# Four head pairs of the first batch: keys transposed unscaled, their inverse norm given to the exponential

## The chip, the core and the metric

The kernel runs on one core of one Trainium2 chip. The metric is the device time of one launch in microseconds (us); 597.22 us is the median of five runs of the kernel before. The core has a matrix engine (TensorE, PE in the profile; PEld is its weight load), a vector engine (VectorE, DVE), a scalar engine (ScalarE, ACT), GpSimd (POOL) and SyncE (SP). Each works through its own instructions in order; semaphores make one wait for another. POOL and SP issue the DMA transfers here.

## What is computed

Cosine attention over 8 batches, 12 heads, 448 tokens and 64 numbers a head, followed by a mixer: a low-rank mix over the tokens and a two-layer perceptron of width 3072.

```python
q_n = q / (norm(q) + 1e-06);  k_n = k / (norm(k) + 1e-06)
attn = softmax(q_n @ k_n.T / tau)            # tau = 0.1
x = (attn @ v) as [8, 448, 768]
u = x + (x.T @ U @ V).T                      # rank 32 over the tokens
out = u + relu(u @ w_ch1) @ w_ch2
```

## The kernel before

The work is planned at build time. `Plan` (L100) holds a list of operations, each with an engine, an estimated duration, what it depends on, the buffer slots that it takes and gives back, and a priority. `plan.run` (L153) plays them in estimated time, and the order in which they come out is the order in which the instructions stand on each engine. So a different duration or priority in one place can reorder the engines' instructions elsewhere. PE and POOL have streams whose order is kept; ACT, DVE and SP take the ready operation of lowest priority number. Where the plan sees PE idle, the last loop (L963) puts in small matmuls on a dummy tile (`warm_up`, L547), which compute nothing that is used.

Heads go in pairs, six to a batch. For each group of heads:

- `load_qk` (L463) brings q and k from HBM, cast to bf16, with the 448 tokens laid out as 112 partitions x 4 chunks. For batch 0 there are four groups: heads 0-1 (float32, through SP, L906), heads 2-3, 4-7 and 8-11 (through POOL, L909 to L913). `load_v` (L472) brings v in four transfers. On POOL the order is heads 2-3, 4-7, the identity matrix for transposing, v, heads 8-11, then weights.
- `squares` (L482) squares q and k on ACT or DVE (L495, L497) and DVE sums each row of 64 (L501).
- `scales` (L508) makes 1/(norm + eps): ACT takes Ln (L514) and Exp of half of it (L517), DVE adds eps (L520) and takes the reciprocal (L522).
- `norm` (L552) multiplies q and k by it on DVE (L564, into `xn`), PE transposes both in `flip` (L434; four transposes of 112x128 for q, four for k, L446), and ACT or DVE copies the transposed tiles to `qkT` (L852, L854).
- `attention` (L585): per pair four chunks of 112 keys. For each, PE computes two score matmuls, one per head (L599), into two PSUM banks; one Exp over both, 896 wide, with the constant scale 1/tau, writes `attn` (L605). When all four are there, 32 matmuls per pair multiply with v (L619); v carries a column of ones, so the row sums come along. DVE divides (L626, L628) into X. `attn` has two buffers.

When batch 0's attention is complete, `stage0` and `columns` (L662, L640) do the low-rank mix and the transposition to `uT` (L676, L650, L655), and `mlp` (L767) starts with the matmuls of L788 and then L822. The first layer of batch 0 waits for the last exponential of batch 0 (L791). From then on, the perceptron's matmuls of one batch fill PE around the attention of the following batches.

U and V of the mix are loaded in float32 through SP after the first pair is normalised (L876, L922), and cast to bf16 on POOL (L882, L885). POOL's casts stand in its queue ahead of the q and k loads of batch 1.

Of the kernel before, what the change touches and what calls it, by code (L numbers as in the profile page):

```python
# [12 lines left out]
BF = mybir.dt.bfloat16  # L13
# [8 lines left out]
PAD = 64  # L22
# [234 lines left out]
def kernel(  # L257
# [24 lines left out]
    G = 4  # L282
    inv_tau = 1.0 / float(tau)
    EPS = 1e-6
    PE_BATCHES = 2
    LATE, VLATE = 8.0, 3.2
    BURST = 2
    FILL = 0.7

# [19 lines left out]
    xn_t = fixed(3, [SCH, 2 * SC, 128], BF, "xn")  # L309
    attn_t = fixed(2, [SCH, SC, 2, 512], BF, "attn")  # L310
    v_t = fixed(2, [SCH, H, SC, D + 2], BF, "v_nat")
# [73 lines left out]

    plan = Plan()
    pe_warm = plan.stream("PE")
    pe_tp = plan.stream("PE")
# [72 lines left out]
    last_av = {}  # L461

    def load_qk(b, h0, h1, ld=None, lo=0, uses=None):  # L463

        ld = ld or Slot(r_ld, 4 if uses is None else uses)
        ops = [load(lambda i=i, src=src: nc.gpsimd.dma_start(  # L466
            out=ld.tile[:, i, lo:lo + h1 - h0, :],
            in_=src[b, h0:h1].rearrange("h (s c) d -> s h (c d)", c=SC)),
            (h1 - h0) * (0.31 if b else 0.35) + (1.2 if b == 0 and h0 == 4 and i == 0 else 0.0), acq=[ld], late=2.5 if b == 0 else LATE) for i, src in enumerate((q, k))]
        return ld, ops, lo  # L470

    def load_v(b):  # L472

        old = [last_av.get((b - 2, p)) for p in range(NPAIR)]
        ops = [load(lambda c=c: nc.gpsimd.dma_start(  # L475
            out=v_t[b % 2][:, :, c, 0:D],
            in_=v[b].rearrange("h (s c) d -> c s h d", c=SC)[c]),
            SCH * H * (0.001 if b else 0.0009), deps=old, late=LATE if b else VLATE) for c in range(SC)]
        for h in range(H):
            got[b, h, "v"] = ops  # L480
# [27 lines left out]
    def scales(b, h0, h1, ld, ops, lo, ii, inv, pr, on, hold=(), then=()):  # L508

        g = h1 - h0  # L510
        ss, ln, nv = Slot(r_ss, 1), Slot(r_ln, 1), Slot(r_ln, 1)
        red = squares(b, g, ld, ops, lo, ii, ss, pr, on, hold, then)
        w = slice(ii[0], ii[-1] + 1)
        o = plan.add(Op("ACT", 0.25, lambda: nc.scalar.activation(  # L514
            ln.tile[:, w, 0:g, :], ss.tile[:, w, 0:g, :], AF.Ln),
            deps=red, acq=[ln], rel=[ss], prio=0))
        up = o = plan.add(Op("ACT", 0.2, lambda: nc.scalar.activation(  # L517
            nv.tile[:, w, 0:g, :], ln.tile[:, w, 0:g, :], AF.Exp, scale=0.5),
            deps=[o], acq=[nv], rel=[ln], prio=0))
        o = plan.add(Op("DVE", 0.21, lambda: nc.vector.tensor_scalar_add(  # L520
            nv.tile[:, w, 0:g, :], nv.tile[:, w, 0:g, :], EPS), deps=[o], prio=pr))
        o = plan.add(Op("DVE", 0.27, lambda: nc.vector.reciprocal(  # L522
            inv.tile[:, w, 0:g, :], nv.tile[:, w, 0:g, :]), deps=[o], acq=[inv], rel=[nv], prio=pr))
        return o, up

    def stats(b, h0, h1, ld, ops, lo, hold=(), then=()):

        pr = 0.3 + 0.03 * h0 if b == 0 else 4
        inv = Slot(r_inv, h1 - h0)
        o, _ = scales(b, h0, h1, ld, ops, lo, (0, 1), inv, pr, "DVE" if b else "ACT/DVE", hold, then)  # L530
        for p in range(h0 // 2, h1 // 2):
            o_ = norm(b, p, ld, lo + 2 * p - h0, inv, 2 * p - h0, {0: o, 1: o}, pr)
        return o_

    def stats_first(ld, ops):

        inv = Slot(r_inv, 2)
        done, ups = {}, []
        for i in range(2):
            done[i], up = scales(0, 0, 2, ld, ops, 0, (i,), inv, -1 - 0.1 * i, "ACT")  # L540
            ups.append(up)
        return ups + norm(0, 0, ld, 0, inv, 0, done, -1)

# [7 lines left out]

    def norm(b, p, ld, la, inv, a, deps, pr):  # L552


        by_pe = b < PE_BATCHES
        first = b == 0 and p == 0
        xn, qkT = Slot(r_xn, 2 if by_pe else 1), Slot(r_qkT, SC // (1 if b == 0 else BURST))

        def part(i):
            def fn():  # L560
                src = ld.tile[:, i, la:la + 2, :].rearrange("p h (c d) -> p h c d", d=D)
                sc = inv.tile[:, i, a:a + 2, :].unsqueeze(3).to_broadcast([SCH, 2, SC, D])
                dst = xn.tile[:, SC * (1 - i):SC * (2 - i), :].rearrange("p c (h d) -> p h c d", h=2)
                nc.vector.tensor_mul(dst, src, sc)  # L564
            return plan.add(Op("DVE", dve_t(512), fn, deps=[deps[i]], acq=[xn],
                               rel=[getattr(ld, "slot", ld), inv], prio=pr))

        ops = {i: part(i) for i in ((0, 1) if first else (1, 0))}
        if not by_pe:
            done = [plan.add(Op("SP", 0.1, lambda: nc.sync.dma_start_transpose(  # L570
                out=qkT.tile, in_=xn.tile.rearrange("p b e -> p (b e)")), deps=list(ops.values()), acq=[qkT],
                rel=[xn], prio=0, lat=("x", 0.05 * 56, LATE)))]
        else:
            done = []
            for i, o in ops.items():
                b0, b1 = SC * (1 - i), SC * (2 - i)
                done.append(flip(
                    pe_tp, [(lambda z=z: xn.tile[:, z, :]) for z in range(b0, b1)], SCH,
                    lambda: qkT.tile, (lambda t_, x, b0=b0, b1=b1: [(t_[:, b0:b1, :], x)]),
                    [o], [qkT], [xn], 1, "ACT/DVE", 0.05))  # L580
        got[b, p, "qkT"] = (qkT, done)
        return list(ops.values())


    def attention(b, p, X):  # L585
        off = PAD * (b % 2)
        qkT, qdeps = got.pop((b, p, "qkT"))
        attn = Slot(r_attn, 2)
        exps = []
        g = 1 if b == 0 else BURST  # L590
        for c0 in range(0, SC, g):
            scs = [Slot(r_sc, 1) for _ in range(g)]

            def score(scs=scs, c0=c0):
                flat = qkT.tile.rearrange("p b s -> p (b s)")
                for n, sc in enumerate(scs):
                    for hh in range(2):
# [5 lines left out]
                            deps=qdeps, acq=scs, rel=[qkT]), pe_first if b == 0 else pe_sc)  # L603
            for n, sc in enumerate(scs):
                exps.append(plan.add(Op("ACT", act_t(2 * S, 0.08), lambda sc=sc, c=c0 + n: nc.scalar.activation(  # L605
                    out=attn.tile[:, c, :, off:off + S], in_=sc.tile[0:SCH, :, 0:S], func=AF.Exp,
                    scale=inv_tau), deps=[o], acq=[attn], rel=[sc], prio=0.1 if b == 0 else 1)))
        last_exp[b] = exps[-1]
# [256 lines left out]
    warm_set = fill(lambda: nc.vector.memset(warm_t, 1.0), 128, prio=-20)  # L865
    plan.add(Op("PE", 5.4, lambda: warm_up(52), deps=[warm_set], acq=[warm]), pe_warm)
    attn_set = [fill(lambda t_=t_: set_attn(t_), 1000, prio=i - 2.5) for i, t_ in enumerate(attn_t)]
# [13 lines left out]
    def cast_u(par):  # L881
        nc.gpsimd.tensor_copy(out=U_sb[:, par], in_=U_f()[:, par])  # L882

    def cast_v():
        nc.gpsimd.tensor_copy(out=V_sb[:, PAD:PAD + S].rearrange("r (c s) -> r c s", c=SC),  # L885
                       in_=V_f().rearrange("r (s c) -> r c s", c=SC))
# [11 lines left out]
    def att(b):  # L898
        X = Slot(r_X, 0) if b else X0
        muls = [] if b else list(muls0)  # L900
        for p in range(0 if b else 1, NPAIR):
# [8 lines left out]
    third = load_qk(0, 4, 8)  # L910
    id_set = plan.add(Op("POOL", 0.8, lambda: make_identity(nc, ident)), pool_q)
    load_v(0)
    fourth = load_qk(0, 8, 12)  # L913
    v_set = [fill(lambda: set_v(v_t[0]), 1000, prio=-1.4)]
# [3 lines left out]
    begun_2 = stats(0, 2, 4, *second, hold=begun[:2], then=begun)  # L918
    z = fill(lambda: nc.vector.memset(V_sb, 0.0), 500, prio=3, deps=begun)
    zf = fill(lambda: nc.vector.memset(U_f(), 0.0), 400, prio=0.5, acq=[uv], deps=begun)  # L920
    u0 = load_u(0)
# [7 lines left out]
    v_set.append(fill(lambda: set_v(v_t[1]), 1000, prio=3, deps=late))  # L929
    consts = [plan.add(Op("POOL", 0.4, lambda: cast_u(0), deps=u0 + [z], rel=[uv]), pool_q),  # L930
              plan.add(Op("POOL", 1.2, cast_v, deps=v0 + [z], rel=[uv]), pool_q),
              plan.add(Op("POOL", 0.4, lambda: cast_u(1), deps=u1 + [z], rel=[uv]), pool_q)]
    state[0] = att(0)
# [29 lines left out]
    for o in order:  # L963
        if o.by == "PE" and not cool:
            if free is not None and o.start - free > 0.25:
                warm_up(int((o.start - free - 0.12) * FILL / 0.056))
            free, cool = o.start + o.dur, warm in o.rel
        for s in o.acq:
            if s.tile is None and not getattr(s, "own", False):
                s.tile = s.ring.make(s.group if isinstance(s.ring, BankRing) else s.i)  # L970
        o.fn()
# [33 lines left out]
```

## Time and profile before

| what | value |
|---|---|
| five runs | 597.95, 597.39, 596.33, 596.21, 597.22 us; median 597.22 |
| the profiled execution's own time | 595.37 us |
| its span in the profile | 593.6 us |
| PE busy | 585.7 us (99%) |
| DVE / ACT / POOL busy | 308.2 (52%) / 270.2 (46%) / 75.9 us (13%) |
| dummy matmuls (L550) | 195, of which 188 start before 32 us |
| granted TensorE clock | 1.00 |

In what follows a timeline line reads: start, time taken, engine, line of the code, operation, tile written <- tiles read, how often; in brackets, the idle time of the engine before it and what ended it. A line that stands for several instructions in a row gives the time from the first start to the last end. A line of windows gives the stretch and its length and then, for each engine, busy microseconds and the number of instructions. A busy PE says little by itself: matmuls overlap, and the dummy ones count.

### The profile page before, as it was taken

The numbers are of one execution on the slowest core, as the hardware profiler recorded it, in microseconds if no ns is written. First come the engines' busy times: TensorE is split into PE (matmuls) and PEld (weight loads), VectorE is DVE, ScalarE is ACT, GpSimd is POOL, SyncE is SP. The second block draws the span as 40 slices with busy tenths as digits, with TensorE's granted clock in tenths as the row PEclk, the third lists the DMA queues.
The fourth block names the chain that finished last, engine by engine and source line by source line (L and its number), as shares of the span: only waits on it lengthen the run. The fifth ranks groups of instructions, "written<-read, shape, count | busy, mean of one in ns | idle before, by whom it ended". The sixth has DMA issues, their size and how long they took to land.

```text
span 593.6 us, 11746 instructions
## 1 busy us (share of the span) xinstructions
PE 585.7 (99%) x4920; PEld 333.2 (56%) x4920; DVE 308.2 (52%) x729; ACT 270.2 (46%) x425; POOL 75.9 (13%) x101
## 2 busy tenths in 40 slices
PE   8999999999999999999999999999999999999997
PEld 7665655444555555554445655465445666554565
DVE  7969949999987768658772442224221210110011
ACT  7777753566555576447661156505631025014300
POOL 6354220040400210130020000000000000000000
PEclk9999999999999999999999999999999999999999
DMA  9999993897996595695494131121002110510021
GB/s 152 196 190 188 210 167 76 129 141 93 110 153 121 76 96 90 129 136 77 48 78 95 42 59 32 41 67 29 1 1 66 45 37 0 94 41 0 1 55 53
DMA packets 132852, 50.68 MB, mean 85 GB/s; under 512 B 97728, under 2 KB 132800, under 8 KB 132800
## 3 DMA queue, kind: packets, MB, share of 16 engines
q0 software_dynamic: 71680, 25.73, 38.9%
q1 hardware_dynamic: 61056, 24.19, 20.8%
q8 instruction: 38, 0.62, 0.4%
q14 instruction: 14, 0.11, 0.1%
q10 hardware_dynamic: 64, 0.02, 0.0%
HBM read 52.25 MB, written 11.01 MB: 107 GB/s over the span
## 4 chain that ended last, share of the span: by engine, by line
PE 93%; DVE 3%; POOL 1%; DMA 1%; ACT 1%; issue 0%; DVEq 0%; POOLq 0%
PE bank L788 38%; PE bank L822 37%; PE bank L619 8%; PE bank L599 7%; PE bank L712 2%; DMA qk_nat<-in_q_dram 1%; DVE xn L564 1%; ACT attn L605 1%; PE bank L676 1%; PE bank L446 1%; POOL v_nat L475 1%; POOL qk_nat L466 0%; DVE ss L501 0%; DVE u_nat L726 0%; DVE O_sb L831 0%
## 5 line engine op out<-in xcount | busy, mean ns | idle before, releaser
L788 PE MATMUL bank<-uT,w_sb 128*128 128x512 bf16 (+1 forms) x1152 | 232.9, 353 | 0.2 <-ACT uT L852 0.2
L822 PE MATMUL bank<-w_sb,relu 128*128 128x384 bf16 (+1 forms) x1368 | 230.7, 323 | 0.3 <-DVE O_sb L831 0.3
L605 ACT ACTIVATE attn<-bank 112x896 bf16<-112x896 f32 x192 | 166.1, 915 | 126.7 <-PE bank L599 82.4
L822 PEld LDWEIGHTS <-relu 128*128 128x128 bf16 x1368 | 129.3, 98 | 92.7 <-issue 13.4
L788 PEld LDWEIGHTS <-w_sb 128*128 128x128 bf16 x1152 | 108.4, 98 | 110.5 <-issue 17.1
L811 ACT ACTIVATE relu<-bank 128x384 bf16<-128x384 f32 (+1 forms) x138 | 75.2, 545 | 131.8 <-PE bank L788 130.9
L831 DVE TENSOR_TENSOR O_sb<-bank,u_nat 128x384 f32<-128x384 f32 (+1 forms) x57 | 31.1, 549 | 173.1 <-PE bank L822 158.6
L501 DVE TENSOR_REDUCE ss<-sq 112x8 f32<-112x512 bf16 x96 | 62.9, 674 | 2.9 <-ACT sq L495 2.7
L619 PEld LDWEIGHTS <-attn 112*128 112x128 bf16 x1536 | 56.1, 97 | 10.4 <-issue 3.4
L564 DVE TENSOR_TENSOR xn<-qk_nat,inv 112x512 bf16<-112x512 bf16 x94 | 61.2, 680 | 0.2
L619 PE MATMUL bank<-v_nat,attn 112*128 112x65 bf16 x1536 | 59.4, 193 | 0.4 <-DMA v_nat<-in_v_dram 0.4
L599 PE MATMUL bank<-qkT 64*128 64x448 bf16 x384 | 54.9, 355 | 0.3 <-ACT attn L605 0.2
L813 DVE TENSOR_SCALAR relu<-bank 128x384 bf16<-128x384 f32 (+1 forms) x54 | 33.5, 622 | 32.8 <-PE bank L788 32.0
L628 DVE TENSOR_TENSOR X_sb<-bank,rd 128x256 bf16<-128x256 f32 x96 | 39.2, 417 | 1.3
L626 DVE RECIPROCAL rd<-bank 128x4 f32<-128x4 f32 x96 | 16.5, 176 | 44.0 <-PE bank L619 43.7
L475 POOL DMA_DIRECT2D v_nat<-in_v_dram x32 | 29.9, 940 | 52.9 <-PE bank L619 49.8
L466 POOL DMA_DIRECT2D qk_nat<-in_q_dram x24 | 17.1, 714 | 149.3 <-DVE xn L564 137.9
L497 DVE TENSOR_TENSOR sq<-qk_nat 112x512 bf16<-112x512 bf16 x89 | 34.3, 416 | 0.2
L726 DVE TENSOR_TENSOR u_nat<-bank,X_sb 128x384 bf16<-128x384 f32 (+2 forms) x45 | 22.4, 525 | 15.9 <-PE bank L712 15.5
L599 PEld LDWEIGHTS <-qkT 64*128 64x128 bf16 x384 | 12.0, 94 | 22.1 <-issue 18.5
L466 POOL DMA_DIRECT2D qk_nat<-in_k_dram x24 | 16.8, 702 | 5.0 <-DMA w_sb<-in_moe_w_ch_dram 4.2
L550 PE MATMUL bank<-warm 128*128 128x128 bf16 x195 | 16.0, 244 | 1.1 <-DVE warm L865 1.1
(49 smaller groups left out, 153.4 us busy)
## 6 DMA issues: line engine op xcount, KB each, us to landing
v_nat<-in_v_dram POOLq DMA_DIRECT2D x32, 168.0 KB, 6.2
qk_nat<-in_q_dram POOLq DMA_DIRECT2D x23, 224.0 KB, 5.3
qk_nat<-in_k_dram POOLq DMA_DIRECT2D x23, 224.0 KB, 6.2
w_sb<-in_moe_w_ch_dram POOLq DMA_DIRECT2D x4, 1152.0 KB, 15.3
w_sb<-in_moe_w_ch_dram POOLq DMA_DIRECT2D x8, 576.0 KB, 16.2
out_dram<-O_sb SPq DMA_DIRECT2D x15, 168.0 KB, 2.2
out_dram<-O_sb SPq DMA_DIRECT2D x16, 144.0 KB, 2.1
out_dram<-O_sb SPq DMA_DIRECT2D x16, 120.0 KB, 2.0
```

The source lines that it names most:

```text
L466: ops = [load(lambda i=i, src=src: nc.gpsimd.dma_start(out=ld.tile[:, i, lo:lo + h1 - h0, :], in_=src[b, h0:h1].rearrange("h (s c) d -> s ...
L475: ops = [load(lambda c=c: nc.gpsimd.dma_start(out=v_t[b % 2][:, :, c, 0:D], in_=v[b].rearrange("h (s c) d -> c s h d", c=SC)[c]), SCH * H ...
L497: nc.vector.tensor_mul(y, x, x)
L501: lambda i=i, a0=a0, a1=a1, sq=sq: nc.vector.reduce_sum(ss.tile[:, i, a0:a1, :].rearrange("p h c -> p (h c)"), sq.tile[:, 0:a1 - a0, :].re ...
L564: nc.vector.tensor_mul(dst, src, sc)
L599: nc.tensor.matmul(out=sc.tile[:, hh, 0:S], lhsT=flat[r, SCH * (c0 + n):SCH * (c0 + n) + 128], rhs=qkT.tile[r, SC:2 * SC, :].rearrange("p ...
L605: exps.append(plan.add(Op("ACT", act_t(2 * S, 0.08), lambda sc=sc, c=c0 + n: nc.scalar.activation(out=attn.tile[:, c, :, off:off + S], in_ ...
L619: nc.tensor.matmul(out=av.tile[:, t, 0:D + 1], lhsT=attn.tile[:, j, hh, 128 * t:128 * (t + 1)], rhs=v_t[b % 2][:, h, j, 0:D + 1], start=(j ...
L628: muls.append(plan.add(Op("DVE", dve_t(256), lambda av=av, rd=rd, h=h: nc.vector.tensor_mul(X.tile[:, :, h * D:(h + 1) * D], av.tile[:, :, ...
L788: o = plan.add(Op("PE", pe_t(n), lambda cc=cc: nc.tensor.matmul(out=mm.tile[:, 0:n], lhsT=w1_sb[:, cc, f * 128:(f + 1) * 128], rhs=uT.tile ...
L811: nc.scalar.activation(out=relu.tile[:, f, 0:n], in_=mm.tile[:, 0:n], func=AF.Relu)
L822: nc.tensor.matmul(out=mm.tile[:, 0:c1 - c0], lhsT=relu.tile[:, f, i * 128:(i + 1) * 128], rhs=w2_t[:, f, c0:c1], start=(f == 0), stop=(f ...
```

## The change

Only the batch 0 part of the code and the shared rings are touched.

1. For pairs 0 to 3 of batch 0 (`RAW_KEYS`) the keys are no longer multiplied by their inverse norm. PE transposes them as loaded; for pair 0, which is loaded in float32, one copy casts them to bf16 first. For pairs 1 to 3 PE reads the loaded tile, in which a head is 64 wide, so there are eight transposes of 112x64 in place of four of 112x128.
2. The inverse norm of the keys becomes the scale of the exponential: each row of scores is one key, so the scale is a column of numbers, one per partition. It differs between the two heads of a pair, so each Exp of 896 becomes two of 448. The factor 1/tau is split: q and k each get 1/sqrt(tau) in the reciprocal step.
3. Ln and Exp of `scales` are one planned operation (as are the two DVE steps behind it), and in the first pair the key's row sum is ordered behind the normalising of q.
4. POOL issues the loads of heads 8-11 ahead of v.
5. `attn` has three buffers.
6. U and V are cast on DVE, not POOL; two of the clearing memsets move to the start.
7. Planning numbers change: `plan.safe` is 0.1 until batch 0's attention is planned (0.25 before), the estimated load times differ, 31 dummy matmuls open the kernel in place of 52, and the filler formula counts a slower PE before 7 us.

```diff
+    RAW_KEYS = {(0, 0), (0, 1), (0, 2), (0, 3)}
...
-    attn_t = fixed(2, [SCH, SC, 2, 512], BF, "attn")
+    attn_t = fixed(3, [SCH, SC, 2, 512], BF, "attn")
...
+        def inverse():
+            nc.vector.tensor_scalar(nv.tile[:, w, 0:g, :], nv.tile[:, w, 0:g, :], EPS, root_tau,
+                                    op0=ALU.add, op1=ALU.mult)
+            nc.vector.reciprocal(inv.tile[:, w, 0:g, :], nv.tile[:, w, 0:g, :])
...
+        def raw():
+            c = Op("ACT/DVE", any_t(512), None, deps=loaded[1], acq=[xn], rel=[ld.slot], prio=-0.9)
+            c.fn = lambda: copy_op(
+                c, xn.tile[:, 0:SC, :].rearrange("p c (h d) -> p h c d", h=2),
+                ld.tile[:, 1, la:la + 2, :].rearrange("p h (c d) -> p h c d", d=D))
+            return plan.add(c)
+
+        keys = (b, p) in RAW_KEYS
+        ops = {0: part(0), 1: raw()} if first and keys else {0: part(0)} if keys else {
+            i: part(i) for i in ((0, 1) if first else (1, 0))}
...
+                ins = [(lambda z=z: xn.tile[:, z, :]) for z in range(b0, b1)] if i in ops else [
+                    (lambda c=c, hh=hh: ld.tile[:, 1, la + hh, D * c:D * c + D]) for c in range(SC) for hh in range(2)]
...
+                if (b, p) in RAW_KEYS:
+                    for hh in range(2):
+                        exps.append(plan.add(Op("ACT", act_t(S, 0.08), lambda sc=sc, c=c0 + n, hh=hh: nc.scalar.activation(
+                            out=attn.tile[:, c, hh, off:off + S], in_=sc.tile[0:SCH, hh, 0:S], func=AF.Exp,
+                            scale=inv.tile[:, 1, a + hh, c:c + 1]), deps=[o, scaled], acq=[attn],
+                            rel=[sc, inv], prio=0.1)))
+                    continue
...
-    plan.add(Op("PE", 5.4, lambda: warm_up(52), deps=[warm_set], acq=[warm]), pe_warm)
+    plan.add(Op("PE", 3.4, lambda: warm_up(31), deps=[warm_set], acq=[warm]), pe_warm)
...
-        nc.gpsimd.tensor_copy(out=U_sb[:, par], in_=U_f()[:, par])
+        nc.vector.tensor_copy(out=U_sb[:, par], in_=U_f()[:, par])
...
+    fourth = load_qk(0, 8, 12)
     load_v(0)
-    fourth = load_qk(0, 8, 12)
...
-                warm_up(int((o.start - free - 0.12) * FILL / 0.056))
+                cold = max(0.0, min(o.start, 7.0) - free)
+                warm_up(int(cold * 0.85 / 0.107 + max(0.0, o.start - max(free, 7.0) - 0.12) * FILL / 0.056))
```

## The prediction

> **What bounds it now.** I read first the chain that ended last, then the windows by stage, then the timeline of the first 41 us.
>
> ```profile
> span 593.6 us, 11746 instructions
> PE 93%; DVE 3%; POOL 1%; DMA 1%; ACT 1%; issue 0%; DVEq 0%; POOLq 0%
> 0.00:41.00 41.00, 37.09 (x524) 27.68 (x525) 31.59 (x84) 32.34 (x54) 21.34 (x32) 1.00 1.27 177
> 41.00:100.00 59.00, 58.51 (x559) 34.32 (x558) 47.80 (x117) 33.79 (x57) 14.86 (x20) 1.00 1.25 168
> 100.00:200.00 100.00, 100.00 (x884) 53.37 (x882) 89.91 (x217) 55.24 (x87) 20.09 (x26) 1.00 0.95 119
> ```
>
> The second line is the chain by engine: PE sets 93%. The windows (PE, PEld, DVE, ACT, POOL, granted clock, DMA) show PE full from 41 us on, with 0.5 us idle in the next 59 and none in the 100 after. There another engine can only lose time. The change keeps all matmuls of that part (1152 of the first perceptron layer, 1368 of the second, 384 scores, 1536 with v), so it acts through the moment at which the perceptron's unbroken run begins. This is 40.85:
>
> ```profile
> 9.43 1.71 ACT L605 ACTIVATE attn<-bank 112x896 bf16<-112x896 f32 x2
> 17.31 0.63 ACT L495 ACTIVATE sq<-qk_nat 112x512 bf16<-112x512 bf16 x1
> 19.55 0.53 ACT L852 COPY qkT<-bank 128x448 bf16<-128x448 bf16 x1 [1.62 <-PE bank L446]
> 22.43 1.73 ACT L605 ACTIVATE attn<-bank 112x896 bf16<-112x896 f32 x2
> 28.23 7.65 ACT L605 ACTIVATE attn<-bank 112x896 bf16<-112x896 f32 x9 [0.29 <-PE bank L599]
> ...
> 34.97 1.96 ACT L605 ACTIVATE attn<-bank 112x896 bf16<-112x896 f32 x2
> 40.85 5.68 PE L788 MATMUL bank<-uT,w_sb 128*128 128x384 bf16 x34 [0.24 <-ACT uT L852]
> ```
>
> The 24 exponentials of batch 0 run from 9.43 to 36.93 (34.97 + 1.96); the last lets the perceptron start. ACT's work in these 27.5 us: nine exponentials take 7.65 and one 0.92, so one follows another after (7.65 - 0.92) / 8 = 0.841, and 24 are 20.2; three squares of 0.63 are 1.9; three copies of 0.53 are 1.6; four small Ln and Exp of some 0.23 are 0.9. Sum 24.6. Only 2.9 us are idle, most of it from 17.9 to 22.4, where DVE (full there) has not yet normalised pair 2. So DVE's relief can win at most these 2.9 us, and then ACT binds.
>
> **The change, part by part.**
>
> *Start.* From the changed program's order, with rows of before: DVE sums q's squares at 4.32 as before, casts the raw key (0.4 to 0.7, by the bf16 square of 0.42 and the float32 product of 0.69), has q's inverse norm at 6.01 and normalises q to 6.74; 0.24 later PE transposes (0.36), DVE copies (0.38), and the first scores start near 8.0 (8.88 before). But the exponential now waits for more on ACT: the key's row sum ends at 7.38 (before 5.71), Ln and Exp end at 7.88, and behind them stand the two squares of pair 1, 2 x 0.63, which before were done by 7.27. First exponential at 9.2: 0.2 gained, not 0.9.
>
> *ACT behind it.* 8 wide exponentials 8 x 0.841 = 6.7; squares 1.9; copies 1.6 (three again); six Ln and Exp 1.4, pair 1's now among them: 11.6. To this come 32 halves, 448 wide with a scale read from a tile. No row has such an instruction. Low end: two casts 384 wide in a row start 0.38 apart, so 512 elements more cost 0.46, 448 fewer save 0.40, and a half follows after 0.841 - 0.40 = 0.44. By the durations of single casts (0.48 for 384 wide, 0.27 for 128) an element costs 0.82 ns and 448 save 0.367: 0.47, if the scale costs nothing. High end: no overlap with the instruction before, the wide one alone less half its elements, 0.917 - 0.367 = 0.55. Nearest in form is the copy of 448 numbers from PSUM, alone 0.53. Between this and 0.55 I take 0.54: that an instruction with an operand more to fetch overlaps as well as the others is the weaker guess. So 32 x 0.54 = 17.3, and the last exponential ends at 9.2 + 11.6 + 17.3 = 38.1, against 36.93: +1.2. Walked through queue by queue, no wait is left in this: pair 2 starts at 9.2 + 16 x 0.54 + 1.9 + 1.6 + 1.4 = 22.7 (before 22.43), and by then DVE, which loses three products of 0.65, has pair 2 and 3 ready at 21. At 0.47 the same walk leaves 0.5 us waiting for pair 3's q (its transposes stand behind 16 matmuls with v) and ends at 9.2 + 11.6 + 15.0 + 0.5 = 36.3: -0.6. At 0.44: 0.9 of waits, 35.8: -1.1.
>
> A rule speaks against the change here. The Trainium skill, "ScalarE: Activation LUTs" (What ACT_TABLE_LOAD costs), says that an activation with immediate scale and bias takes 186 ns plus 0.833 ns an element, that each per-partition pointer operand adds about 93 ns, and that neighbours overlap by about 93 ns. The trace agrees for immediates (0.917 for 896 wide, 0.841 apart); no run here shows a pointer yet. By it a half would follow after 0.56, and the end of the exponentials would lie at 38.7, +1.8.
>
> *After the last exponential.* Before, PE needs 3.9 us to 40.85: 32 matmuls with v (1.0), 11 of L650 (0.6), 4 of L655 and 4 of L788 (1.3), 8 of L676 (0.3), 3.3 in all, and bubbles. The changed order leaves two more of L655 and four more of L650 behind the last exponential, 2 x 0.163 + 4 x 0.056 = 0.55. The bubbles may take part of it: 0 to 0.55, I take +0.3.
>
> *Hidden.* PE's 12 more transposes net (84 + 24 for 96), 0.05 each, fall into time that dummy matmuls fill. v is now issued 1.4 us later (two issues of 0.70 ahead of it) and lands behind two more transfers:
>
> ```profile
> v_nat<-in_v_dram POOLq DMA_DIRECT2D x1, 168.0 KB, 7.0
> qk_nat<-in_q_dram POOLq DMA_DIRECT2D x1, 224.0 KB, 6.9
> qk_nat<-in_k_dram POOLq DMA_DIRECT2D x1, 224.0 KB, 7.3
> ```
>
> The last v lands at 7.44 + 7.0 = 14.4, the two loads behind it at 15.3 and 16.4, about 1 us apiece, so v comes near 16.6. PE reaches the first matmul with v at about 20, behind the transposes of pair 2, whose scales come that late; 3.5 us of cover, and were it gone, each us late would delay pair 3's transposes and the exponentials alike. The third buffer takes the place that the later reading of pair 0's would block; before, nothing waited for one. The heads 8-11 arrive 4 us earlier but are not used earlier: DVE is at 15.9 before it squares them. The casts cost DVE 3 x 0.1 to 0.7 (the cast of 128x512 takes 0.69), between 27 and 33, where in its 40 us row it is 57% busy; batch 1's loads leave POOL's queue earlier, behind v, and hold up nothing of batch 0. After 41 us: 0, within 0.5 either way for the other interleaving.
>
> *Sum.* -0.2 (start) + 1.4 (ACT behind it: 28.9 for 27.5) + 0.3 = +1.5 us. On the profiled execution: span 593.6 + 1.5 = 595.1, time 595.37 + 1.5 = 596.9. That execution was 1.85 under the median of the runs, so for a median: 597.22 + 1.5 = 598.7.
>
> **Rivals.**
>
> *Halves as cheap as immediates (not slower).* Place: L628. At 0.44 to 0.47 the exponentials end at 35.8 to 36.3; with the tail, -0.8 to -0.3: 596.4 to 596.9. It decides below the half at which 9.2 + 11.6 + 32 h + 0.3 = 36.93, h = 0.49. For it: Exp and plain copies show the same fixed part (0.917 - 0.735 = 0.18; 0.53 - 0.367 = 0.16, at 0.82 ns an element), so an operand more may cost little. Against it: those are all immediates.
>
> *PE stays slow for longer (slower).* The dummy matmuls run at two speeds:
>
> ```profile
> 4.00:5.00 1.00, 1.00 (x13) 1.00 (x11) 0.69 (x1) 0.91 (x2) 0.93 (x4) 1.00 0.83 85
> 5.00:6.00 1.00, 1.00 (x12) 1.00 (x11) 0.95 (x4) 0.65 (x4) 1.00 (x2) 1.00 1.19 144
> 7.00:8.00 1.00, 1.00 (x21) 0.92 (x18) 0.97 (x3) 0.65 (x2) 1.00 (x2) 1.00 1.32 168
> ```
>
> 12 or 13 in a us to 6, 21 from 7, at the same granted clock; before, PE is unbroken from 1.06 to 7.39. Now 41 in a row end near 5.4, and 0.4 us later come the first transposes. If that gap puts off the faster speed to 10 or 14 us, the 36 fillers and transposes that stand before scores of pair 0 cost 0.05 more each; half lies under ACT's backlog: +0.9, with the sum 599.6; to 20 us, 600.7. Against it: the gap is small. The skill, "TensorE: Matmul & The Clock Gate" (What's actually happening), has a free-running activity window of 3.4 us that must be busy; the speed-up near 6.6 fits two windows, and a miss by one would put it at 10.
>
> *More won than counted (faster).* The plan's new interleaving closes small gaps later: PE needs some 550 us for what single rates (0.163 for 384 wide, 0.217 for 512) put near 537. A tenth of that is -1.3, with cheap halves -1.9: 595.3. Against it: PE's waits after 41 us come to 0.7 us in all.
>
> *No shift.* DVE relief and dearer halves cancel, 597.2 to 597.7; this is the forecast with h at 0.49 to 0.51.
>
> **How the numbers follow.** What can be told from no change in this kernel is about 0.2%, 1.2 us. Forecast (+0.7 to +2.4, h 0.52 to 0.55, with the tail's and the later bounds): 50%, of which 35 above 1.2 and 15 below. Cheap halves: 23%, of which 10 beyond -1.2 with the later half us, 13 within. Slow PE: 12%, slower. More won: 11%, faster. No shift: 4%. Slower 0.47, same 0.32, faster 0.21. The forecast alone: 597.9 to 599.6. The range reaches to h = 0.44 with 0.8 more won, 595.5, and to the slow PE, 600.7.
>
> **What would show it.** ACT's first exponential at 9.2 behind two squares; the median of one 448 wide Exp near 0.54 or above and the interval in a row of 8; pair 2 at 22.7, the last exponential ending at 38.1, the long run of L816 starting at 42.4; PE's waits after it as before. Wrong if halves follow each other under 0.49, if ACT idles between 9.2 and 38, if a matmul with v waits for DMA, or if PE's time from the start of the run to the end differs by over 1 us from 552.8 (593.6 - 40.85).

## The result, and the profile after

| | median | runs | ratio to before (95%) |
|---|---|---|---|
| before | 597.72 us | 88 | |
| changed | 598.56 us | 47 | 1.0018 (1.0013 to 1.0023) |

The changed kernel is slower by about 1.1 us by the ratio; the two medians differ by 0.84. The profiled execution took 599.59 us (span 597.8), 1.0 over its median, as that of before was 2.4 under its own (595.37 for 597.72): the 4.2 us between the two spans are no measure of the change, and what in them belongs to one execution has to be told from what belongs to the program.

The chain by engine, and the same windows as before (PE, PEld, DVE, ACT, POOL, granted clock, DMA share, GB/s):

```profile
PE 92%; DVE 4%; ACT 2%; DMA 1%; issue 0%; POOL 0%; DVEq 0%; POOLq 0%
```

```profile
0.00:41.00 41.00, 36.05 (x472) 23.59 (x472) 30.28 (x84) 34.20 (x67) 19.62 (x30) 0.96 1.33 187
41.00:100.00 59.00, 57.24 (x547) 33.35 (x547) 45.89 (x107) 34.26 (x58) 16.08 (x21) 1.00 1.22 163
100.00:200.00 100.00, 99.83 (x887) 53.71 (x886) 90.75 (x218) 54.90 (x88) 18.66 (x24) 1.00 0.90 115
```

PE was full from 41 us on before. Now 1.8 us are missing between 41 and 100 (part of them is the later start) and 0.2 in the 100 after. In the first 41 us the granted clock is 0.96, no longer 1.00.

The timeline of ACT and the start of PE's long run:

```profile
9.82 1.68 ACT L628 ACTIVATE attn<-bank,inv 112x448 bf16<-112x448 f32 x3 [0.93 <-PE bank L620]
...
22.76 8.49 ACT L628 ACTIVATE attn<-bank,inv 112x448 bf16<-112x448 f32 x16
31.03 6.69 ACT L633 ACTIVATE attn<-bank 112x896 bf16<-112x896 f32 x8
39.06 1.63 ACT L880 CAST uT<-bank 128x384 bf16<-128x384 f32 x4 [1.35 <-DVE X_sb L656]
...
43.02 3.73 PE L816 MATMUL bank<-uT,w_sb 128*128 128x384 bf16 x22 [0.57 <-ACT uT L880]
```

Sixteen halves in a row take 8.49 us; one alone takes 0.656, so one follows another after (8.49 - 0.656) / 15 = 0.522. The last exponential ends at 31.03 + 6.69 = 37.72, and the long run starts 5.30 later. Before, these were 36.92 and 3.93.

Three stretches can be read in every profile: the opening up to the end of batch 0's last exponential, the tail from there to the long run, and the rest to the end of the span. Two executions of the kernel before and the experiments below give:

| program | last exponential ends | tail | rest | span |
|---|---|---|---|---|
| before, first profile | 36.92 | 3.93 | 552.75 | 593.6 |
| before, second profile (e8) | 39.42 | 3.93 | 552.75 | 596.1 |
| changed | 37.72 | 5.30 | 554.78 | 597.8 |
| changed, same PE order (e2) | 36.42 | 5.30 | 554.78 | 596.5 |

Tail and rest agree to a hundredth between two executions with one PE order: they belong to the program. What varies is the opening. Taking tail, rest and the 1.75 us between span and time from the medians gives the opening of a usual execution, worked out and not read from a trace: before 597.72 - 1.75 - 552.75 - 3.93 = 39.3, changed 598.56 - 1.75 - 554.78 - 5.30 = 36.7. So in a usual execution the change wins 2.6 us in the opening, loses 1.4 in the tail and 2.0 in the rest: +0.8, the difference of the medians.

### The profile page after: what moved, and what is told of

The parts are those of the page before. It is cut to its first block, busy times and chain, and to the rows that moved or that the text cites. A ratio compares the mean times of both kernels' runs of the same rounds, so it can differ in the third digit from the quotient of the medians.

```text
span 597.8 us, 11650 instructions
## 1 busy us (share of the span) xinstructions
PE 586.8 (98%) x4878; PEld 330.0 (55%) x4878; DVE 308.8 (52%) x730; ACT 272.3 (46%) x441; POOL 74.0 (12%) x98
## 4 chain that ended last, share of the span: by engine, by line
PE 92%; DVE 4%; ACT 2%; DMA 1%; issue 0%; POOL 0%; DVEq 0%; POOLq 0%
PE bank L850 37%; PE bank L816 36%; PE bank L647 8%; PE bank L620 7%; PE bank L740 1%; ACT attn L628 1%; DMA qk_nat<-in_k_dram 1%; PE bank L448 1%; DVE xn L573 1%; PE bank L704 1%; PE bank L559 1%; DVE u_nat L754 1%; DVE relu L841 0%; DVE O_sb L859 0%; DVE u_nat L790 0%
## 5 line engine op out<-in xcount | busy, mean ns | idle before, releaser
L633 ACT ACTIVATE attn<-bank 112x896 bf16<-112x896 f32 x176 | 152.7, 921 | 123.8 <-PE bank L620 84.0
L839 ACT ACTIVATE relu<-bank 128x512 bf16<-128x512 f32 (+1 forms) x139 | 75.7, 545 | 130.8 <-PE bank L816 129.6
L573 DVE TENSOR_TENSOR xn<-qk_nat,inv 112x512 bf16<-112x512 bf16 x91 | 59.2, 678 | 0.1
L620 PE MATMUL bank<-qkT 64*128 64x448 bf16 x384 | 57.8, 356 | 0.9 <-ACT qkT L880 0.6
L501 DVE TENSOR_TENSOR sq<-qk_nat 112x512 bf16<-112x512 bf16 x89 | 34.1, 414 | 0.0
L628 ACT ACTIVATE attn<-bank,inv 112x448 bf16<-112x448 f32 x32 | 17.4, 656 | 0.9 <-PE bank L620 0.9
```

Of the source, the lines that this page charges most:

```text
L501: nc.vector.tensor_mul(y, x, x)
L620: nc.tensor.matmul(out=sc.tile[:, hh, 0:S], lhsT=flat[r, SCH * (c0 + n):SCH * (c0 + n) + 128], rhs=qkT.tile[r, SC:2 * SC, :].rearrange("p ...
L839: nc.scalar.activation(out=relu.tile[:, f, 0:n], in_=mm.tile[:, 0:n], func=AF.Relu)
```

## The experiments

**e1: the scale made a constant.** The keys' inverse norm is left out for pairs 0 to 3; the order on PE and ACT stays that of the changed kernel.

```diff
-                            scale=inv.tile[:, 1, a + hh, c:c + 1]), deps=[o, scaled], acq=[attn],
+                            scale=10.0), deps=[o, scaled], acq=[attn],
```

> The changed kernel in the same order, but the 32 half exponentials of pairs 0 to 3 take the constant 10 as their scale, so the keys' inverse norm is left out there. Theory A (the scale read from a tile is what makes a half follow after 0.52 us, and ACT sets the end of the opening): a half alone falls from 0.656 to about 0.55, the interval in a row of 16 from 0.52 to 0.45, the last exponential ends some 1.5 us earlier, the median falls from 598.6 to about 597.2. Rival B (PE's scores, fillers and matmuls with v set the pace between 25 and 37 us in the profile of the changed kernel): a half alone falls as well, but the interval stays above 0.50 and the median within 0.4 of 598.6.

596.23 us, ratio to before 0.9977 (0.9968 to 0.9986): 2.3 us under the changed kernel. ACT's groups in the changed kernel up to 60 us, then ACT's timeline with the constant scale:

```profile
L628 ACT ACTIVATE attn<-bank,inv 112x448 bf16<-112x448 f32 x32 | 17.4, 656 | 0.9 <-PE bank L620 0.9
```

```profile
20.32 7.03 ACT L628 ACTIVATE attn<-bank 112x448 bf16<-112x448 f32 x16
27.29 6.80 ACT L633 ACTIVATE attn<-bank 112x896 bf16<-112x896 f32 x8
```

With the constant, one half alone has a mean of 562 ns, and in a row they follow after (7.03 - 0.562) / 15 = 0.431. So the operand read from a tile costs 0.094 alone and 0.091 in a row: nothing of it is hidden by the overlap. 32 x 0.091 = 2.9 us on ACT; the last exponential ends at 34.09 against 36.42 in e2, and the 2.3 us arrive whole in the median. Theory A, with more than the 1.5 it expected.

**e2: U and V loaded later.**

```diff
-    zf = fill(lambda: nc.vector.memset(U_f(), 0.0), 400, prio=-1.35, acq=[uv])
+    zf = fill(lambda: nc.vector.memset(U_f(), 0.0), 400, prio=0.5, acq=[uv], deps=begun)
```

> The changed kernel, but the memset of the U region stands again behind the first row sums, so that SP's loads of U and V start after 8 us and not at 1.92. Every other instruction keeps its place. Theory A (these loads take DMA time from the keys of pair 1, whose transposes held up the first scores to 9.24): the keys of heads 2-3 land near 6.7 in place of 8.3, the first exponential starts at 9.2 in place of 9.8, the PE clock does not drop to 0.5 at 8 to 11, and the median falls by 0.6 to 1.2, to 597.4 to 598.0. Rival B (ACT has slack behind, or the two squares hold the first exponential anyway): the landing moves, the median stays within 0.3 of 598.6.

598.39 us, ratio 1.0016 (1.0006 to 1.0026): as the changed kernel, Rival B. In the changed kernel's profile SP's loads had started at 1.92 and PE waited 1.21 us for the keys of pair 1:

```profile
8.29 0.58 PE L448 MATMUL bank<-ident,qk_nat 112*64 112x112 bf16 x8 [1.21 <-DMA qk_nat<-in_k_dram]
```

In e2 those keys land at 7.0 and the first exponential comes at 8.59; but in e1, where SP's loads also start at 1.92, they land at 6.7 and it comes at 8.58. So the late landing was one execution's; that the early loads cause it in some executions is possible and not shown.

**e3: no raw keys.**

```diff
-    RAW_KEYS = {(0, 0), (0, 1), (0, 2), (0, 3)}
+    RAW_KEYS = set()
```

> The changed kernel with no pair in the set of raw keys: all keys are normalised, all exponentials are 896 wide; loads, memsets, three buffers, casts on DVE and planning numbers as changed. Theory A (the halves cost more than DVE's relief brings): faster than the changed kernel by about 1, 597.6. Rival B (the relief is worth more than the halves, and what made the kernel slower are the other edits): slower than the changed kernel, 599.5 or more.

597.86 us, ratio 1.0006 (0.9996 to 1.0016): 0.7 under the changed kernel, between the two expectations and nearer to A. Its first exponential comes at 10.85, two us later than in e2, and still the last ends at 36.17, 0.25 earlier: its last 15 wide ones follow each other after 0.83, two halves after 1.04. Tail 5.30 is that of the changed kernel and rest 554.5 nearly so (554.78): the tail does not come from the raw keys, nor, with this allowance, does the rest.

**e4: two attn buffers.**

```diff
-    attn_t = fixed(3, [SCH, SC, 2, 512], BF, "attn")
+    attn_t = fixed(2, [SCH, SC, 2, 512], BF, "attn")
```

> The changed kernel with two attn buffers. Theory A (with v later, pair 2's exponentials would wait for pair 0's matmuls with v): slower by 0.5 to 1.5, 599.1 to 600. Rival B (the third buffer changes only the interleaving after 42 us, in which the profile of the changed kernel lost 2 us): same or faster, 597.5 to 598.6.

601.82 us, ratio 1.0070 (1.0056 to 1.0084): 3.3 over the changed kernel, more than A's. The last exponential ends at 37.84 (1.4 later than e2), tail 5.70, rest 556.2. The wait that Theory A named does not show: pair 2's exponentials begin at 21.52, in e2 at 21.48. But the plan's order is another one: two copies (L880, 0.53 each) stand on ACT between the eighth and the ninth of the last sixteen halves, which are 1.2 us apart there and follow without a break in e2. So the 3.3 us are the price of the plan made for two buffers; what a missing buffer costs by a wait is not shown.

**e5: the plan's allowance as before.**

```diff
-    plan.safe = 0.1
+    plan.safe = 0.25
```

> The changed kernel with plan.safe at 0.25 in batch 0, as before the change. Its PE order has four of the low-rank mix's matmuls (L683) and their transposes ahead of pair 5's matmuls with v, where the changed kernel has them behind. Theory A (the smaller allowance made the plan put them behind, and this is why the changed kernel needs 5.30 us from the last exponential to the long run of L816, against 3.92 before): 3.9 to 4.3 us there, median lower by 1.0 to 1.4, 597.2 to 597.6. If the 2 us that the changed kernel loses later against the profile of before come from the same number, 595.5. Rival B (the tail is set by the chain of v, division, transposes and copies, whatever the order): 5 us or more there, median 598.2 to 598.8.

596.06 us, ratio 0.9976 (0.9966 to 0.9985): 2.5 under the changed kernel, and faster than both. PE around the last exponential (ends at 37.72) in the changed kernel, then in e5 (ends at 36.88):

```profile
37.55 1.31 PE L647 MATMUL bank<-v_nat,attn 112*128 112x65 bf16 x32
38.70 0.33 PE L683 MATMUL bank<-V_sb,A_sb 128*128 128x384 bf16 x1
38.86 0.33 PE L678 MATMUL bank<-ident,X_sb 128*128 128x128 bf16 x3
...
41.15 0.34 PE L683 MATMUL bank<-V_sb,A_sb 128*128 128x384 bf16 x1
...
42.11 0.34 PE L683 MATMUL bank<-V_sb,A_sb 128*128 128x384 bf16 x1
```

```profile
35.98 0.33 PE L683 MATMUL bank<-V_sb,A_sb 128*128 128x384 bf16 x1
36.14 0.33 PE L678 MATMUL bank<-ident,X_sb 128*128 128x128 bf16 x3
36.31 0.33 PE L683 MATMUL bank<-V_sb,A_sb 128*128 128x384 bf16 x1
...
36.72 0.33 PE L683 MATMUL bank<-V_sb,A_sb 128*128 128x384 bf16 x1
37.01 1.18 PE L647 MATMUL bank<-v_nat,attn 112*128 112x65 bf16 x32
...
40.36 1.95 PE L816 MATMUL bank<-uT,w_sb 128*128 128x384 bf16 x11
```

With the allowance of 0.25 the mix's matmuls that need only earlier pairs run while PE would wait for the last exponential, and the tail is 3.48. With 0.1 the plan has pair 5's matmuls with v first. The kernels without raw keys show the same: 5.30 at 0.1 (e3), 3.92 at 0.25 (e7). Why the plan chose so, that the allowance stands between an exponential's planned end and PE, is read from the code and not shown. The rest is 553.94, 0.8 less than in the changed kernel. Theory A for the tail; the further gain in the rest is under half of the 2 us hoped for.

**e6: e5 with raw keys in pairs 0 and 1 alone.**

```diff
-    RAW_KEYS = {(0, 0), (0, 1), (0, 2), (0, 3)}
+    RAW_KEYS = {(0, 0), (0, 1)}
```

> As e5_safe_025, with raw keys in pairs 0 and 1 alone: 16 half exponentials fewer, eight wide ones more, two key products more on DVE. Theory A (ACT binds): 16 x 0.522 - 8 x 0.841 = 1.6 us less on ACT, and the last exponential ends up to 1.6 earlier than in e5. Rival B (DVE's two products come back into the wait for pair 2): the exponentials of pair 2 start later than in e5 by more than 0.5, and the last ends within 0.5 of e5's.

596.96 us, ratio 0.9994 (0.9982 to 1.0006). The last exponential ends at 36.30, 0.6 before e5's, which lies between the theories; the tail is 4.57 for 3.48 and takes it back.

**e7: e5 without raw keys.**

```diff
-    RAW_KEYS = {(0, 0), (0, 1), (0, 2), (0, 3)}
+    RAW_KEYS = set()
```

> As e5_safe_025, with no raw keys at all: it tells what the raw keys are worth when the order behind them is the one of before. Theory A (halves and relief cancel, as e3 and the changed kernel suggest: last exponential at 36.2 and 36.4): median within 0.5 of e5's. Rival B: e5 is faster by 1 or more, since its first exponential comes 2 us earlier.

598.07 us, ratio 1.0015 (1.0004 to 1.0026): 2.0 over e5, Rival B, against e3, which says the opposite at the other allowance. The opening accounts for 0.5 of it (37.34 for 36.88), the tail for 0.4 (3.92), the rest for 1.0 (554.94). So most of the difference is order again, and the worth of the raw keys by themselves stays open: from -2.0 to +0.7 by the plan around them.

**e8: the kernel before, a second profile** (the same file).

> The kernel before, once more, for a second profile. Theory A (the 552.8 us from the start of the long run of the first perceptron layer to the end belong to its order of instructions, and the changed kernel's 554.8 to its own): 552.5 to 553.2 again. Rival B (the first profiled execution, at 595.37 the fastest but one of all runs, was a lucky one): 554 or more.

597.82 us, the usual time. The rest is 552.75 as in the first profile: Theory A. What differs is the opening: the last exponential ends 2.5 us later. Its DMA landing for q of heads 8-11, DVE's timeline there, and ACT's:

```profile
qk_nat<-in_q_dram POOLq DMA_DIRECT2D x1, 224.0 KB, 8.7
```

```profile
17.12 0.76 DVE L497 TENSOR_TENSOR sq<-qk_nat 112x512 bf16<-112x512 bf16 x2 [1.90 <-DMA qk_nat<-in_q_dram]
```

```profile
24.93 1.73 ACT L605 ACTIVATE attn<-bank 112x896 bf16<-112x896 f32 x2
27.07 3.37 ACT L605 ACTIVATE attn<-bank 112x896 bf16<-112x896 f32 x4 [0.41 <-PE bank L599]
30.73 8.69 ACT L605 ACTIVATE attn<-bank 112x896 bf16<-112x896 f32 x10 [0.29 <-PE bank L599]
```

The transfer took 8.7 us from issue to landing, in the first profile 6.9. DVE's order has the squares of heads 8-11 ahead of pair 2's normalising, so it stood 1.9 us and squared them 1.80 later (17.12 for 15.32), and pair 2's exponentials began at 24.93 instead of 22.43.

The other 0.7 of these 2.5 us is lost on DVE as well, beside POOL's cast of V. DVE's four products of that stage in the first profile, then both in the second:

```profile
18.41 2.57 DVE L564 TENSOR_TENSOR xn<-qk_nat,inv 112x512 bf16<-112x512 bf16 x4
```

```profile
20.21 3.28 DVE L564 TENSOR_TENSOR xn<-qk_nat,inv 112x512 bf16<-112x512 bf16 x4
21.11 1.24 POOL L885 CAST V_sb<-raw_uv 128x448 bf16<-128x448 f32 x1 [2.23 <-DMA raw_uv<-in_moe_V_dram]
```

The third product began at 21.41, during that cast, and took 1.49 us in place of 0.68; it ended 0.55 after the cast. Three more products began during a cast on POOL and ended 0.54 to 0.55 after it: one in the first profile, one in e9's, and one in e12's, which again took 1.48. The change moves these casts to DVE; no run tries that by itself.

The clock fell too: it was 0.50 from 16.94 to 20.36, after PE had stood 1.4 us for v, which landed late as well. The 41 dummy matmuls ahead of pair 2's transposes took 3.59 us for 2.46, and the transposes began 0.50 after their product was done, in the first profile 0.06. In this execution DVE came later still, so the slow clock added nothing that shows.

**e9: before, with only the loads swapped.**

```diff
-    load_v(0)
     fourth = load_qk(0, 8, 12)
+    load_v(0)
```

> The kernel before, with one edit: POOL issues the loads of heads 8-11 ahead of v. The orders on DVE, ACT and SP stay as they were. In the second profile of the kernel before, DVE stood 1.9 us for q of heads 8-11, whose squares stand ahead of pair 2's normalising, and pair 2's exponentials began at 24.9 instead of 22.4. Theory A (the load order is what the change wins in a usual execution): that wait is gone, pair 2's exponentials begin near 22.4 and the median falls by 1 to 2.5, to 595.2 to 596.7. Rival B (v, now later, holds pair 0's matmuls with v, which in this kernel stand ahead of pair 1's last scores): PE waits for v by 1 us or more, and the median stays within 0.7 of 597.6 or rises.

596.61 us, ratio 0.9985 (0.9972 to 0.9998), tail 3.92 and rest 552.77 as before. The wait for heads 8-11 is gone, but PE waits 1.2 us for v, the clock is 0.50 from 17.95 to 21.36, and pair 2 starts at 24.2: both theories have a part. The swap is worth 0.9 us by itself (interval 0.1 to 1.7), and the clock divides it: five executions with a mean clock of 0.999 or 1.00 took 595.1 to 596.2, seven with 0.997 took 596.5 to 597.4.

**e10: the changed kernel with v first.**

```diff
-    fourth = load_qk(0, 8, 12)
     load_v(0)
+    fourth = load_qk(0, 8, 12)
```

> The changed kernel with v issued ahead of heads 8-11, as before the change; the order behind the last exponential stays that of the changed kernel. Theory A (the load order carries most of what the change wins): pair 2's exponentials begin 1.5 us or more later than the 21.5 of e2, and the median rises by 1 to 2.5, to 599.6 to 601. Rival B (with DVE relieved, heads 8-11 are not needed earlier): median within 0.7 of 598.6.

597.62 us, ratio 1.0006 (0.9994 to 1.0018): 0.9 under the changed kernel, which neither theory expected. The opening ends at 36.25 (e2 36.42): it is no longer with v first, as Rival B has it. But the load order is not all that differs: DVE's order is another from 16.7 us on and ACT's from 20.9, behind the last exponential too. The rest is 553.75 for 554.78, and this 1.0 is the whole difference.

**e11: e5 with the half's price in the plan.**

```diff
-                        exps.append(plan.add(Op("ACT", act_t(S, 0.08), lambda sc=sc, c=c0 + n, hh=hh: nc.scalar.activation(
+                        exps.append(plan.add(Op("ACT", act_t(S, 0.15), lambda sc=sc, c=c0 + n, hh=hh: nc.scalar.activation(
```

> As e5_safe_025, and the plan is told 0.15 in place of 0.08 for the fixed part of a half exponential, which is what the trace shows in a row (0.522 less 0.372). Theory A (a plan that knows the half's price orders the engines better): 0.3 to 1 faster than e5, 595.0 to 595.8. Rival B (the order is right already): within 0.4 of 596.06.

596.66 us, ratio 0.9990 (0.9979 to 1.0001): 0.6 over e5, neither theory. The run starts at 40.12 (e5 40.36); the rest is 554.38, 0.44 more. So the profiles explain 0.2 of the 0.6.

**e12: before, with a third attn buffer alone.**

```diff
-    attn_t = fixed(2, [SCH, SC, 2, 512], BF, "attn")
+    attn_t = fixed(3, [SCH, SC, 2, 512], BF, "attn")
```

> The kernel before with a third attn buffer alone. Theory A (the third buffer pays only where the exponentials run ahead of the matmuls with v, as in the changed kernel, where taking it away cost 3.3): within 0.7 of 597.6. Rival B (it is worth 1 us or more by itself): 596.6 or less.

597.48 us, ratio 1.0001 (0.9985 to 1.0017): Theory A. Its profile is one of a late opening (39.84, tail 3.93), as e8's.

## Why the prediction was right in its sum and wrong in its terms

The forecast was slower by 1.5 us, at 598.7; measured are 1.1 and 598.56. The direction rests on two causes of the right kind, the dearer half exponential and the work left behind the last one. The terms, by the usual execution worked out above:

| step of the prediction | predicted | measured |
|---|---|---|
| half exponential in a row | 0.54 us | 0.522 |
| last exponential ends, before | 36.93 | 39.3 |
| last exponential ends, changed | 38.1 | 36.7 |
| tail | +0.3 (0 to 0.55) | +1.37 |
| rest | 0 (-0.5 to +0.5) | +2.03 |

*The half exponential* was right in mechanism and size: taken at 0.54 by the rows nearest in form, against 0.47 if the operand were free, it is 0.522; without the operand e1 has 0.431. The Trainium skill, "ScalarE: Activation LUTs" (What ACT_TABLE_LOAD costs), gave 93 ns for a pointer operand; e1 shows 94 alone and 91 in a row. The rival of cheap halves has its time, too: with them e1 is faster than before by 0.2%.

*The start of the opening.* In the profile the first exponential came at 9.82, 0.6 after the predicted 9.2, because the first scores stood behind pair 1's late keys; in e2 it came at 8.59. The two squares of pair 1 do stand ahead of it, as predicted. The profile's later numbers then lie near the predicted ones (pair 2 at 22.76 for 22.7, last end 37.72 for 38.1), but the execution was late by that accident: e2 has 21.48 and 36.42. Against e2 the predicted 38.1 is 1.7 too late: 0.6 at the first exponential (8.59 for 9.2), 0.6 in the 32 halves (0.522 for 0.54), 0.5 in the rest of ACT's work.

*The step that failed on the opening* is "The heads 8-11 arrive 4 us earlier but are not used earlier". It fits the changed kernel (e10 ends its opening as early with v first) and was wrong of the one before: its DVE used them at 15.32, and they had landed at 8.38 + 6.9 = 15.28. A wait with no slack is a wait in any execution in which the transfer takes longer, and the second profile of before loses 1.8 us there, and 0.7 where a product meets POOL's cast of V. The prediction has the casts as a cost on DVE alone; that on POOL they can hold up DVE's products it did not see. The chain of the first profile had the piece of DMA in it; it was read as 1% and left. So "DVE's relief can win at most these 2.9 us" was set against the wrong opening. Which edit wins the 2.6 us is not shown: without raw keys (e3) and with v first (e10) the opening ends as early, and the move of the casts was not tried alone.

*The tail.* Counting the matmuls behind the last exponential (its list adds to 3.2 us, not 3.3) gave 0.55 us more and "the bubbles may take part of it". But PE's work was not the measure: casts of A and uT stand between its matmuls there (ACT's wait of 1.35 before the uT casts, PE's of 0.57 before the run), and work placed behind 32 matmuls starts that chain later. e5 moves the same work in front and the tail falls from 5.30 to 3.48. The cause is an edit that the prediction listed as a planning number and never priced, plan.safe.

*The rest* was put at 0, and what would show it wrong was named: PE's time from the run's start to the end off by over 1 us from 552.8. It is 554.8. PE's longest waits after 41 us in the changed kernel:

```profile
PE bank L816 <- ACT uT L880: 0.6, 1, 0.6
PE bank L816 <- DVE qkT L882: 0.5, 1, 0.5
PE bank L816 <- DVE u_nat L751: 0.5, 1, 0.5
PE bank L850 <- DVE O_sb L859: 0.3, 1, 0.3
PE bank L816 <- DVE u_nat L754: 0.3, 1, 0.3
PE bank L816 <- DVE relu L841: 0.3, 1, 0.3
```

The first stands ahead of the run and is part of the tail. The others, with one of 0.2, are 2.1 us, 1.6 more than before's 0.5 there; so most of the 2.0 is waits for DVE in the new interleaving. Which edit made them is not settled: plan.safe at 0.25 takes away 0.8, v first 1.0, and without raw keys the rest falls by 0.2 at one allowance and rises by 1.0 at the other.

*The rival of a slower PE* came about in the profiled execution, though not from the start: the clock in it fell at 8 us, as shown below, and its first scores took 0.93 us for four where e2 needs 0.56. e2 and e1 keep the few dummy matmuls and have full clock throughout. In the changed kernel it is rare and does not explain the median: 6 of its 47 executions have a mean clock of 0.997, which is what 3.41 us at half clock leave of 597, and 41 have 0.999 or 1.00. It is the kernel before that has it often: of the 90 executions beside the experiments, 44 have a mean clock of 0.997 or less and took 597.0 to 599.0, 46 have more and took 595.4 to 598.1. So a fall of the clock goes with the late opening of before and is not all of it. In e8 it was hidden; what it costs in the median is not shown.

So the sum was right by luck, because errors cancelled: -2.6 in place of +1.2 in the opening, and +3.4 in place of +0.3 behind it.

The best of these kernels is e5, the change with plan.safe left at 0.25: 596.06 us, 0.24% under the kernel before.

## What to carry to other kernels

Where a planner orders the instructions, a number that only feeds it is an edit like any other: compare the order around the last event of the stage, and price what now stands behind it by the chain that it starts, not by its matmuls. Before an edit is costed against a profile, look for transfers that land just as they are used: they are on the path in the next execution. And a per-partition scale in an activation has a price for each instruction, so halving the width to use one pays it twice as often.

## What the runs showed of the hardware

The granted TensorE clock in the changed kernel's profile, then in the second profile of the kernel before (windows cut where the clock changes; the clock is the third number from the end):

```profile
4.58:7.99 3.41, 1.79 (x26) 1.28 (x24) 2.74 (x7) 1.98 (x7) 3.41 (x5) 1.00 1.22 143
7.99:11.40 3.41, 3.11 (x28) 2.05 (x29) 2.45 (x7) 2.46 (x6) 3.41 (x5) 0.50 1.49 198
```

```profile
13.53:16.94 3.41, 1.99 (x34) 1.35 (x34) 1.67 (x3) 2.22 (x5) 0.00 (x0) 1.00 1.54 203
16.94:20.36 3.42, 3.42 (x38) 2.94 (x35) 3.24 (x9) 2.48 (x4) 0.29 (x1) 0.50 1.22 239
```

In the 3.41 us before the fall PE was busy for 1.79 and 1.99 us, and stood for at most 0.92 and 0.99 us on end. The half clock then held for 3.41 us, although PE was full from 9 us on in the first and throughout in the second. e9 and e12 have the same stretch of 3.41 us, after 2.09 and 1.95 us of PE. In all 14 profiles the clock changes on a grid of 3.41 us. Of all the steps of this grid, from the first mark of the clock in a trace to the end of the work, the four with the least PE, 1.79 to 2.09 us or 53 to 61%, are the four that half clock follows; the next one, 2.14 us in e7 (3.82 to 7.23), is followed by full clock, though PE stands 1.27 us on end in it. So what counts in these profiles is PE's busy share of a step, not one gap in it. The Trainium skill, "TensorE: Matmul & The Clock Gate" (What's actually happening), has a free-running window of 3.4 us whose activity sets the clock, and half clock after an idle window; the length agrees, while here PE was busy for over half of the window before.

Landing times differ by execution: the same 224 KB of q took 6.9 us and 8.7 us behind the same queue in two executions of one program, 1.8 us of the 2.5 by which its openings differ, while tail and rest repeat to 0.01 us.

A bf16 product on DVE that begins during a cast on POOL ends 0.54 to 0.55 us after that cast, in all four cases of these profiles, and took up to 1.49 us for 0.68. A row sum on DVE (L501) that began during the cast of V in the first profile kept its 0.67 us.
